# Float64 weights decoded and split between the steps of a three-stage attention and feed-forward kernel

## The chip, the cores and the metric

One core of a Trainium2 chip runs the whole kernel as one program. The metric is device time in microseconds (us). The kernel before took 1129.61 us, median of 3 runs (1129.01 to 1131.65). A profile of one execution of it is what the rows below are from.

## The reference

The inputs are an attention problem (B = 4, H = 8, S = 576, D = 64) and two feed-forward layers on its 2304 x 512 output, each with 512 x 2048 and 2048 x 512 weights (the first layer's `w_in` arrives scaled by 4.32). The weights are float64, so a core that computes in 32 bits has to decode them.

```
local   = softmax(causal(q k^T / 8)) v
mem_out = phi(q) M_prev / (phi(q) z_prev + 1e-6),  phi(x) = x if x > 0 else exp(x) - 1, plus 1
x = sigmoid(beta) * mem_out + (1 - sigmoid(beta)) * local
h = x @ w_in1;  g = h if h >= 1, 0 if h <= -1, else (h + 1)^2 / 4;  x = g @ w_out1
h = x @ w_in2;  g = max(0.01 h, h);                                out = g @ w_out2
```

## The kernel before

All products of the feed-forward layers run on TensorE (PE) in a reduced fp32 format. To keep precision, each operand is split into a high part and a low remainder: ScalarE (ACT) copies the value into the reduced format, VectorE (DVE) subtracts that from the value. Each product is then three matmuls: high x high, high x low, low x high.

A layer's 2048 hidden units do not fit in memory at once, so each layer is computed in two halves of 8 slots of 128 hidden units. That makes four segments (`SEGS`): 0 and 1 are layer 1, 2 and 3 are layer 2. Each segment goes over 9 chunks of 256 tokens (`CHUNKS`, 36 in all). The program counts time in steps: step x = 8n + f is chunk n, slot f. Layer 1 has steps 0 to 143. Layer 2 has a product step for each pair of slots (x = 144, 146, ...). Attention runs interleaved with the first 46 steps; behind it a block (`manual_schedule`) keeps TensorE, ScalarE, VectorE and GpSimd in the order in which the program is written. The DMA queue of SyncE (SP) is ordered by a planner.

A layer 1 step is `mm_h` (12 matmuls, then on ACT a Relu and a Square, L542 and L543, then on DVE the value g, its high part gh and its low part gl, L544 to L546), and `mm_y` of the step two before (`LAG` = 2: 12 matmuls on gh and gl). The last `mm_y` of a chunk is followed by `finish`, in segment 1 with two DVE adds (L569). At f = 5 the next chunk's x is split: `high_x` (L507 on DVE for layer 1, L509 on ACT for layer 2) and `low_x` (DVE, L514).

A layer 2 step is `mm_h2` (24 matmuls, then an ACT copy scaled by 0.01, L589, a DVE maximum, L590, and four DVE sums of 128 columns, L591 to L594, that feed a 7-product form of a 2x2 block multiplication), `layer2_y` of the step two before (21 matmuls, L607 to L609; after the fourth, `finish2` with 7 DVE adds), an ACT copy gh (L735) and the DVE remainder gl (L716).

Weights come as 64-bit integers in tiles `raw` (three buffers, 512 KB each). Decoding half a slot is one ACT operation (L122) and five DVE operations (L123, L127, L129, L130, L132). `split_half` splits a decoded input half (ACT L189, DVE L190). `split_out` first forms four combinations of two output halves on DVE (L204 to L207) and then splits them in two parts of two splits each; one of its temporaries, `t1`, is taken from the two buffers of g.

When all this is done stands in a table of jobs by step: `FETCH` for segment 1 (12 of its 16 decodes at steps 47, 49, ... 69), `HALVES` for segments 2 and 3, and a list of steps for the splits of segments 2 and 3. `do_jobs(x)` stands ahead of `mm_h` in layer 1, so a step's whole decode and its splits are ahead of that step's g in the DVE's queue:

```
for f in range(NSLOT):
    do_jobs(8 * n + f)
    pend.append((n, f, mm_h(n, f)))
```

In layer 2 `do_jobs(x - 1)` stands ahead of `mm_h2` and `do_jobs(x)` ahead of gl.

Of the kernel before, what the change touches and what calls it, by code (L numbers as in the profile page):

```python
# [20 lines left out]
TC = 256  # L21
# [15 lines left out]

BOOT, BOOT0, DELAY = 2.0, 12.0, 1.0

FETCH = {1: [24 + 4 * i for i in range(NW)] + [47 + 2 * i for i in range(16 - NW)]}  # L40
HALVES = {N1: [82 + 7 * i // 2 for i in range(16)], N1 + 1: [x for x in range(150, 209) if x % 8 in (0, 6)]}
HB = 1

# [8 lines left out]
def attn_moe_moe_kernel(ctx, tc, q, k, v, m_prev, z_prev, beta, w1i, w1o, w2i, w2o, out):  # L52
# [73 lines left out]
    def decode_b(lo, dst, a, r):  # L126
        nc.vector.scalar_tensor_tensor(out=a, in0=dst.bitcast(I32), scalar=3, in1=a,  # L127
                                       op0=ALU.logical_shift_left, op1=ALU.bitwise_or)
        nc.vector.tensor_scalar(out=r.bitcast(I32), in0=a, scalar1=-2 ** 23, scalar2=None, op0=ALU.bitwise_and)  # L129
        nc.vector.scalar_tensor_tensor(out=r, in0=lo.bitcast(U32), scalar=2.0 ** -52, in1=r,  # L130
                                       op0=ALU.mult, op1=ALU.mult)
        nc.vector.tensor_tensor(dst, a.bitcast(F32), r, ALU.add)  # L132

    slot_w, phase = {}, []
# [28 lines left out]
    def fetch_halves(seg, halves):  # L163

        ahead = 2 if seg else RAWB
        if any(SEGS[t][0:2] == SEGS[seg][0:2] for t in range(seg)):
            for k, (f, x) in enumerate(halves):
                nc.sync.dma_start(out=new_w32(seg, f, x, k), in_=w_d[f][:, x])
                yield
                yield  # L170
            return
        raws = [load_raw(seg, *h) for h in halves[0:ahead]]
        for k, (f, x) in enumerate(halves):
            if not raws:
                raws = [load_raw(seg, *h) for h in halves[k:k + ahead]]
            w32 = new_w32(seg, f, x, k if seg else 0)
            part = decode_a(raws.pop(0), w32)
            yield
            decode_b(*part)
            if any(SEGS[t][0:2] == SEGS[seg][0:2] for t in range(seg + 1, N1)):  # L180
                nc.sync.dma_start(out=w_d[f][:, x], in_=w32)
            else:
                raws += [load_raw(seg, *h) for h in halves[k + ahead:k + ahead + 1]]
            yield

    slots = {}

    def split(dst, src):
        nc.scalar.activation(dst[:, 0], src, AF.Copy)  # L189
        nc.vector.tensor_tensor(dst[:, 1], src, as_r(dst[:, 0]), ALU.subtract)  # L190

    def split_half(seg, f, x):
        w = wts.tile([128, 2, 512], F32R, tag="io"[x] + str(f), name="io"[x] + str(f))
        split(w, slot_w.pop((seg, f, x)))
        slots[f, x] = w

    def split_out(seg, p):


        a, b = (slot_w.pop((seg, f, 1)) for f in (2 * p, 2 * p + 1))  # L200
        b11, b12, b21, b22 = (x[:, c:c + 256] for x in (a, b) for c in (0, 256))
        t = l2_pool().tile([128, 3, 256], F32, tag="t", bufs=2, name="t")
        t1 = ffn.tile([128, TC], F32, tag="g", bufs=2, name="g")
        nc.vector.tensor_tensor(t1, b12, b11, ALU.subtract)  # L204
        nc.vector.tensor_tensor(t[:, 0], b22, t1, ALU.subtract)
        nc.vector.tensor_tensor(t[:, 1], b22, b12, ALU.subtract)
        nc.vector.tensor_tensor(t[:, 2], t[:, 0], b21, ALU.subtract)  # L207
        wa = wts.tile([128, 2, 512], F32R, tag=f"o{2 * p}", name="wa")
        wb = wts.tile([128, 2, 512], F32R, tag=f"o{2 * p + 1}", name="wb")
        ex = l2_pool().tile([128, 2, 768], F32R, tag=f"ex{p}", name="ex")  # L210
        split(wa[:, :, 0:256], b11)
        split(wb, b)
        yield
        split(wa[:, :, 256:512], t1)
        split(ex, t.rearrange("p i c -> p (i c)"))
        slots["out", p] = (wa, wb, ex)
        yield
# [285 lines left out]

    def high_x(n):
        xh = ffn.tile([128, 4, TC], F32R, tag="xh", bufs=2, name="xh")
        if SEGS[CHUNKS[n][0]][0] == 0:
            nc.vector.tensor_copy(xh, xin[n])  # L507
        else:
            nc.scalar.activation(xh, xin[n], AF.Copy)  # L509
        return xh  # L510
# [17 lines left out]
    def mm_h(n, f):  # L528
        seg, c = CHUNKS[n]
        w = slots[f, 0]  # L530
        xh, xl = xin[n]
        hp = psum()[:, 0:TC] if attended else ps.tile([128, TC], F32, tag="h", bufs=HB, name="h")
        for ct in range(4):
            wh, wl = w[:, 0, 128 * ct:128 * ct + 128], w[:, 1, 128 * ct:128 * ct + 128]
            nc.tensor.matmul(hp, wh, xh[:, ct], start=(ct == 0), stop=False)  # L535
            nc.tensor.matmul(hp, wh, xl[:, ct], start=False, stop=False)  # L536
            nc.tensor.matmul(hp, wl, xh[:, ct], start=False, stop=(ct == 3))  # L537
        g = ffn.tile([128, TC], F32, tag="g", bufs=2, name="g")
        gh = ffn.tile([128, TC], F32R, tag="gh", bufs=GB, name="gh")
        gl = ffn.tile([128, TC], F32R, tag="gl", bufs=GB, name="gl")  # L540

        nc.scalar.activation(g, hp, AF.Relu, bias=0.5, scale=0.5)  # L542
        nc.scalar.activation(g, g, AF.Square)  # L543
        nc.vector.scalar_tensor_tensor(out=g, in0=hp, scalar=1.0, in1=g, op0=ALU.max, op1=ALU.min)  # L544
        nc.vector.tensor_copy(gh, g)  # L545
        nc.vector.tensor_tensor(gl, g, as_r(gh), ALU.subtract)  # L546
        return gh, gl

    def mm_y(n, f, yp, gg):
# [24 lines left out]
    def mm_h2(n, p):  # L574


        ws = slots[2 * p, 0], slots[2 * p + 1, 0]
        xh, xl = xin[n]
        hp = psum()
        for s in range(2):  # L580
            o = hp[:, TC * s:TC * s + TC]
            for ct in range(4):
                wh, wl = ws[s][:, 0, 128 * ct:128 * ct + 128], ws[s][:, 1, 128 * ct:128 * ct + 128]
                nc.tensor.matmul(o, wh, xh[:, ct], start=(s == 0 and ct == 0), stop=False)  # L584
                nc.tensor.matmul(o, wh, xl[:, ct], start=False, stop=False)  # L585
                nc.tensor.matmul(o, wl, xh[:, ct], start=False, stop=(s == 1 and ct == 3))  # L586
        g = l2_pool().tile([128, 8, 128], F32, tag="g2", bufs=2, name="g2")
        h4 = hp.rearrange("p (a t) -> p a t", t=128)
        nc.scalar.activation(g[:, 4:8], h4, AF.Copy, scale=0.01)  # L589
        nc.vector.tensor_tensor(g[:, 0:4], h4, g[:, 4:8], ALU.max)  # L590
        nc.vector.tensor_tensor(g[:, 4], g[:, 0], g[:, 2], ALU.add)  # L591
        nc.vector.tensor_tensor(g[:, 6], g[:, 1], g[:, 0], ALU.subtract)
        nc.vector.tensor_tensor(g[:, 5], g[:, 4], g[:, 1], ALU.subtract)
        nc.vector.tensor_tensor(g[:, 7], g[:, 3], g[:, 5], ALU.subtract)  # L594
        gh = l2_pool().tile([128, 7, 128], F32R, tag="gh2", bufs=2, name="gh2")
        gl = l2_pool().tile([128, 7, 128], F32R, tag="gl2", bufs=2, name="gl2")
        return g, gh, gl
# [49 lines left out]
    def at_step(x, fn, *args):  # L647
        jobs.setdefault(x, []).append((fn, args))


    for seg in range(1, N1):
        x0 = START[seg]
# [1 line left out]
        part = fetch_halves(seg, [h[1:] for h in order])  # L654
        for i, (x, f, io) in enumerate(order):
            at_step(x, split_half, seg, f, io)
            at_step(FETCH[seg][i], next, part)
            at_step(FETCH[seg][i], next, part)
    for seg, xs in HALVES.items():
        part = fetch_halves(seg, [(f, x) for f in range(NSLOT) for x in range(2)])  # L660
        for x in xs:
            at_step(x - 1 if seg > N1 else x, next, part)
            at_step(x, next, part)
    for seg, xs in ((N1, (138, 140, 142, 144, 140, 142, 143.5, 144)), (N1 + 1, (210, 212, 214, 216, 214, 216, 220, 222))):
        for p in range(NSLOT // 2):
            for f in (2 * p, 2 * p + 1):
                at_step(xs[p], split_half, seg, f, 0)
            part = split_out(seg, p)
            at_step(xs[4 + p], next, part)
            at_step(int(xs[4 + p]) + 1, next, part)  # L670
# [16 lines left out]
    def layer1_steps():  # L687
        load_x(0)
        low_x(0, high_x(0))
        for n, (seg, c) in enumerate(CHUNKS):  # L690
            if SEGS[seg][0] == 1:
                break
            for f in range(NSLOT):
# [7 lines left out]
                    load_prev(n)  # L701
                if len(pend) > LAG:
                    layer1_y()
                yield 1

    def layer2_y():
# [9 lines left out]
        nc.vector.tensor_tensor(gl, g[:, 1:8], as_r(gh), ALU.subtract)  # L716

    def layer2():
        for n, (seg, c) in enumerate(CHUNKS):
            if SEGS[seg][0] == 0:  # L720
                continue
            for p in range(NSLOT // 2):
# [12 lines left out]
                nc.scalar.activation(gg[1], gg[0][:, 1:8], AF.Copy)  # L735
                if p == 2 and n + 1 < len(CHUNKS):
                    low_x(n + 1, xh)
                do_jobs(x)
                low_part(*gg)
                pend.append((n, p, gg))  # L740
                if p == 2 and n in again:
                    load_prev(n)
# [21 lines left out]
    def do_boot():  # L764
        while boot_jobs and boot_jobs[0][0] <= done:
            _, kind, f, io = boot_jobs.pop(0)
            with tc.issue_after(scored[0]) if scored[0] is not None else ExitStack():
                if kind == 0:
                    next(first), next(first)
                else:  # L770
                    split_half(0, f, io)

# [7 lines left out]

    with tc.manual_schedule(engines={nc.tensor.engine, nc.scalar.engine, nc.vector.engine, nc.gpsimd.engine}):
        attended = True
        for _ in steps:
            pass
        layer2()
# [25 lines left out]
```

## Time and profile before

| | |
|---|---|
| median of 3 runs | 1129.61 us |
| the profiled execution | 1128.14 us, of which 1126.4 us span from first to last instruction |
| PE busy | 1068.6 us (95%) |
| DVE busy | 913.2 us (81%) |
| ACT busy | 602.3 us (53%) |
| mean granted TensorE clock | 0.978 |

How to read it: busy time is a sum over stages. Attention fills the first 425 us, layer 1 reaches to about 719 us (some of it already beside attention), layer 2 to the end. In a table of stretches each line is a stretch (start:end, length), then busy time and (number of instructions) of PE, PEld (weight loads), DVE, ACT and POOL, then the granted TensorE clock, the DMA share and GB/s. In a timeline a line is start, duration, engine, source line, operation, output<-inputs, shapes, count, and in brackets the idle time before and what ended it. Durations overlap a little: the next independent instruction of an engine can start before the one ahead has ended, so what an instruction costs its queue is the distance from its start to the next start.

### The profile page before, as it was taken

What the parts mean: (1) busy time and instruction counts of PE and PEld (TensorE: products, weight loads), DVE (VectorE), ACT (ScalarE), POOL (GpSimd) and SP (SyncE); (2) the same over time, 40 slices, a digit from 0 to 9 for tenths busy, and PEclk for the clock granted to TensorE, in tenths of its full rate; (3) what the DMA queues carried; (4) which work ended last, traced back from release to release, by engine and by line L of the source; (5) the groups of instructions that cost most, each with busy time, mean ns of one, the idle gap of its engine ahead of it and who ended that gap; (6) DMA issues with size and microseconds to landing.
All of it is one profiled execution on the core that took longest, in us unless ns stands there. A gap on an engine that the chain in (4) does not pass through costs nothing.

```text
span 1126.4 us, 22350 instructions
## 1 busy us (share of the span) xinstructions
PE 1068.6 (95%) x8520; PEld 1008.8 (90%) x8520; DVE 913.2 (81%) x2327; ACT 602.3 (53%) x1368; POOL 29.0 (3%) x28
## 2 busy tenths in 40 slices
PE   5877899999999999999999999899999998999997
PEld 4656777888888889989999999899999998999997
DVE  6698999876677767996887877999998999877766
ACT  6998787666676754463333334544444464334332
POOL 0000000000000000000000000000000000211211
PEclk9887999999999999999999999999999999999999
DMA  6455554443344313431343434123322111311211
GB/s 147 115 158 160 147 143 142 119 115 68 88 93 114 81 34 105 133 113 56 127 136 95 132 113 132 57 76 128 97 95 95 58 38 38 113 57 57 98 53 57
DMA packets 122171, 112.09 MB, mean 100 GB/s; under 512 B 67280, under 2 KB 100048, under 8 KB 122064
## 3 DMA queue, kind: packets, MB, share of 16 engines
q1 hardware_dynamic: 122064, 110.66, 33.3%
q8 instruction: 67, 1.10, 0.4%
q14 instruction: 40, 0.33, 0.1%
HBM read 77.60 MB, written 23.59 MB: 90 GB/s over the span
## 4 chain that ended last, share of the span: by engine, by line
PE 75%; DVE 13%; ACT 5%; DMA 4%; issue 2%; SPq 1%; DVEq 0%; ACTq 0%
PE A L584 6%; PE A L585 6%; PE A L586 6%; PE y L557 4%; PE A L535 4%; PE y L556 4%; PE A L537 4%; PE A L536 4%; PE y L558 3%; PE y L609 3%; PE y L608 3%; PE y L607 3%; PE A L348 2%; PE h L535 2%; PE h L536 2%; PE h L537 2%
## 5 line engine op out<-in xcount | busy, mean ns | idle before, releaser
L584 PE MATMUL A<-xh,i 128*128 128x256 f32 x576 | 164.1, 285 | 0.0
L585 PE MATMUL A<-xl,i 128*128 128x256 f32 x576 | 164.0, 285 | 0.0
L586 PE MATMUL A<-xh,i 128*128 128x256 f32 x576 | 163.9, 285 | 0.0
L735 ACT ACTIVATE gh<-g 128x896 fp32r<-128x896 f32 x72 | 68.6, 953 | 145.5 <-DVE g L594 89.5
L542 ACT ACTIVATE g<-A 128x256 f32<-128x256 f32 x98 | 37.5, 383 | 166.3 <-PE A L537 146.0
L585 PEld LDWEIGHTS A<-xl,i 128*128 128x128 f32 x576 | 111.7, 194 | 0.0
L584 PEld LDWEIGHTS A<-xh,i 128*128 128x128 f32 x576 | 111.7, 194 | 0.0
L586 PEld LDWEIGHTS A<-xh,i 128*128 128x128 f32 x576 | 111.6, 194 | 0.0
L556 PE MATMUL y<-gh,o 128*128 128x256 f32 x384 | 108.0, 293 | 3.8 <-DVE gh L545 2.6
L535 PE MATMUL A<-xh,i 128*128 128x256 f32 x392 | 111.5, 284 | 0.0
L536 PE MATMUL A<-xl,i 128*128 128x256 f32 x392 | 111.3, 284 | 0.0
L537 PE MATMUL A<-xh,i 128*128 128x256 f32 x392 | 111.3, 284 | 0.0
L557 PE MATMUL y<-gl,o 128*128 128x256 f32 x384 | 110.1, 289 | 0.2
L558 PE MATMUL y<-gh,o 128*128 128x256 f32 x384 | 108.8, 286 | 0.0
L716 DVE TENSOR_TENSOR gl<-g,gh 128x896 fp32r<-128x896 f32 x72 | 86.8, 1205 | 19.8 <-ACT gh L735 19.8
L363 ACT ACTIVATE e<-e,mx 128x128 f32<-128x128 f32 (+2 forms) x144 | 84.2, 586 | 21.0 <-DVE mx L360 20.9
L360 DVE CUSTOM_DVE_ANT_0 e<-A,mask 128x384 f32<-128x384 f32 (+4 forms) x126 | 60.4, 483 | 42.7 <-PE A L348 41.5
L589 ACT ACTIVATE g<-A 128x512 f32<-128x512 f32 x72 | 42.8, 594 | 74.8 <-PE A L586 74.7
L556 PEld LDWEIGHTS y<-gh,o 128*128 128x128 f32 x384 | 72.0, 193 | 5.4 <-DVE gh L545 3.2
L535 PEld LDWEIGHTS A<-xh,i 128*128 128x128 f32 x392 | 75.8, 193 | 0.4 <-issue 0.4
L536 PEld LDWEIGHTS A<-xl,i 128*128 128x128 f32 x392 | 75.7, 193 | 0.0
L537 PEld LDWEIGHTS A<-xh,i 128*128 128x128 f32 x392 | 75.7, 193 | 0.0
(249 smaller groups left out, 3369.9 us busy)
## 6 DMA issues: line engine op xcount, KB each, us to landing
raw<-in_moe_w_in_dram SPq DMA_DIRECT2D x32, 512.0 KB, 3.7
raw<-in_moe_w_out_dram SPq DMA_DIRECT2D x32, 512.0 KB, 3.4
qk<-qk SPq DMA_DIRECT2D x64, 144.0 KB, 2.5
xf<-y_d SPq DMA_DIRECT2D x18, 512.0 KB, 4.1
xf<-x_d SPq DMA_DIRECT2D x12, 512.0 KB, 3.9
yp_d<-ys SPq DMA_DIRECT2D x18, 256.0 KB, 2.2
xf<-yp_d SPq DMA_DIRECT2D x9, 512.0 KB, 3.4
y_d<-ys SPq DMA_DIRECT2D x18, 256.0 KB, 2.1
```

The costliest lines, as they stand in the source:

```text
L363: nc.scalar.activation(e[:, 0:w], e[:, 0:w], AF.Exp, bias=mx, scale=-1.0, accum_out=ls[:, h:h + 1])
L535: nc.tensor.matmul(hp, wh, xh[:, ct], start=(ct == 0), stop=False)
L536: nc.tensor.matmul(hp, wh, xl[:, ct], start=False, stop=False)
L537: nc.tensor.matmul(hp, wl, xh[:, ct], start=False, stop=(ct == 3))
L556: nc.tensor.matmul(o, wh, gh, start=(f == 0 and et % 2 == 0), stop=False)
L557: nc.tensor.matmul(o, wh, gl, start=False, stop=False)
L558: nc.tensor.matmul(o, wl, gh, start=False, stop=(f == NSLOT - 1 and et % 2 == 1))
L584: nc.tensor.matmul(o, wh, xh[:, ct], start=(s == 0 and ct == 0), stop=False)
L585: nc.tensor.matmul(o, wh, xl[:, ct], start=False, stop=False)
L586: nc.tensor.matmul(o, wl, xh[:, ct], start=False, stop=(s == 1 and ct == 3))
L716: nc.vector.tensor_tensor(gl, g[:, 1:8], as_r(gh), ALU.subtract)
L735: nc.scalar.activation(gg[1], gg[0][:, 1:8], AF.Copy)
```

## The change

- **Decode in pieces.** `decode_b` yields after each DVE operation, so a decode is five pieces instead of two.
- **Filling.** In the part of layer 1 behind attention (`filling`), decode pieces and the DVE subtraction of `split` are not issued where the job stands. They go on a list (`between`), and `mm_h` takes one of them after each of g, gh and gl; `fill(99)` at the end of the step issues what is left. The ACT copies of splits stay where they were.
- **Steps.** The 12 late decodes of segment 1 move to steps 47 + 3i//2 (47, 48, 50, 51, ... 63). The splits of segment 2 move by up to 4 steps, one combination (p = 2) is done ahead at step 136. `do_jobs(x)` goes behind gl for x up to 146.
- **Combination.** `t1` is written in place over the decoded half; the tile t has three buffers.
- **ScalarE.** The layer 2 activation is one ACT operation (`Prelu`, alpha 0.01) in place of the ACT copy and the DVE maximum. `high_x` of layer 1 is on ACT once attention is over.

```diff
-FETCH = {1: [24 + 4 * i for i in range(NW)] + [47 + 2 * i for i in range(16 - NW)]}
+FETCH = {1: [24 + 4 * i for i in range(NW)] + [47 + 3 * i // 2 for i in range(16 - NW)]}
...
     def decode_b(lo, dst, a, r):
         nc.vector.scalar_tensor_tensor(out=a, in0=dst.bitcast(I32), scalar=3, in1=a,
                                        op0=ALU.logical_shift_left, op1=ALU.bitwise_or)
+        yield
         nc.vector.tensor_scalar(out=r.bitcast(I32), in0=a, scalar1=-2 ** 23, scalar2=None, op0=ALU.bitwise_and)
+        yield
...
+    between, filling = [], False
+
+    def fill(n=1):
+        while between and n:
+            fn, args = between.pop(0)
+            fn(*args)
+            n -= 1
+
     def split(dst, src):
         nc.scalar.activation(dst[:, 0], src, AF.Copy)
-        nc.vector.tensor_tensor(dst[:, 1], src, as_r(dst[:, 0]), ALU.subtract)
+        args = dict(out=dst[:, 1], in0=src, in1=as_r(dst[:, 0]), op=ALU.subtract)
+        if filling:
+            between.append((lambda: nc.vector.tensor_tensor(**args), ()))
+        else:
+            nc.vector.tensor_tensor(**args)
...
-        t1 = ffn.tile([128, TC], F32, tag="g", bufs=2, name="g")
-        nc.vector.tensor_tensor(t1, b12, b11, ALU.subtract)
-        nc.vector.tensor_tensor(t[:, 0], b22, t1, ALU.subtract)
         nc.vector.tensor_tensor(t[:, 1], b22, b12, ALU.subtract)
+        nc.vector.tensor_tensor(b12, b12, b11, ALU.subtract)
+        nc.vector.tensor_tensor(t[:, 0], b22, b12, ALU.subtract)
         nc.vector.tensor_tensor(t[:, 2], t[:, 0], b21, ALU.subtract)
+        combos[seg, p] = b11, b12, b, t
...
-        if SEGS[CHUNKS[n][0]][0] == 0:
+        if SEGS[CHUNKS[n][0]][0] == 0 and not attended:
             nc.vector.tensor_copy(xh, xin[n])
...
         nc.vector.scalar_tensor_tensor(out=g, in0=hp, scalar=1.0, in1=g, op0=ALU.max, op1=ALU.min)
+        fill()
         nc.vector.tensor_copy(gh, g)
+        fill()
         nc.vector.tensor_tensor(gl, g, as_r(gh), ALU.subtract)
+        fill()
...
-        nc.scalar.activation(g[:, 4:8], h4, AF.Copy, scale=0.01)
-        nc.vector.tensor_tensor(g[:, 0:4], h4, g[:, 4:8], ALU.max)
+        nc.scalar.activation(g[:, 0:4], h4, AF.Prelu, alpha=0.01)
...
-    for seg, xs in ((N1, (138, 140, 142, 144, 140, 142, 143.5, 144)), (N1 + 1, (210, 212, 214, 216, 214, 216, 220, 222))):
+    for seg, xs in ((N1, (138, 140, 143, 146, 141, 143.5, 146, 148)), (N1 + 1, (210, 212, 214, 216, 214, 216, 220, 222))):
...
+            if (seg, p) == (N1, 2):
+                at_step(136, combine, seg, p)
...
                 if len(pend) > LAG:
                     layer1_y()
+                fill(99)
                 yield 1
...
-                do_jobs(x)
+
+                if x > 146:
+                    do_jobs(x)
                 low_part(*gg)
+                if x <= 146:
+                    do_jobs(x)
```

## Rows read from the trace of the kernel before

**Rows 1.** The page's first part: busy time, share and instructions by engine.
```profile
PE 1068.6 (95%) x8520; PEld 1008.8 (90%) x8520; DVE 913.2 (81%) x2327; ACT 602.3 (53%) x1368; POOL 29.0 (3%) x28
```

**Rows 2.** Table of stretches: full-rate ones and the three short ones.
```profile
485.00:515.00 30.00, 27.47 (x208) 26.47 (x207) 28.22 (x59) 17.62 (x37) 0.00 (x0) 0.94 0.32 104
515.00:715.00 200.00, 200.00 (x1669) 200.00 (x1668) 155.08 (x338) 71.27 (x167) 0.00 (x0) 1.00 0.34 109
715.00:740.00 25.00, 20.68 (x148) 20.07 (x147) 22.54 (x49) 12.11 (x21) 0.00 (x0) 0.86 0.14 44
740.00:925.00 185.00, 185.00 (x1544) 185.00 (x1544) 171.96 (x367) 83.61 (x119) 0.00 (x0) 1.00 0.26 89
925.00:940.00 15.00, 11.18 (x79) 10.77 (x78) 14.65 (x32) 9.09 (x16) 0.00 (x0) 0.89 0.19 70
```

**Rows 3.** Waits of PE behind attention: waiter <- releaser: us in total, times, longest.
```profile
PE y L609 <- DVE gl L716: 4.2, 1, 4.2
PE h L607 <- DVE ys L634: 3.5, 1, 3.5
PE y L556 <- DVE gh L545: 2.4, 2, 1.5
```

**Rows 4.** Timeline of DVE: one decode and the g of a step.
```profile
459.98 0.42 DVE L123 TENSOR_SCALAR da<-raw 128x512 int32<-128x512 int32 x1
460.51 0.69 DVE L127 SCALAR_TENSOR_TENSOR da<-w32b,da 128x512 int32<-128x512 int32 x1
461.24 0.43 DVE L129 TENSOR_SCALAR dr<-da 128x512 int32<-128x512 int32 x1
...
463.03 0.42 DVE L544 SCALAR_TENSOR_TENSOR g<-A,g 128x256 f32<-128x256 f32 x1
463.55 0.29 DVE L545 CAST gh<-g 128x256 fp32r<-128x256 f32 x1
463.88 0.43 DVE L546 TENSOR_TENSOR gl<-g,gh 128x256 fp32r<-128x256 f32 x1
464.22 0.42 DVE L544 SCALAR_TENSOR_TENSOR g<-A,g 128x256 f32<-128x256 f32 x1
```

**Rows 5.** Groups of instructions by line: count, busy us, mean ns, idle before.
```profile
L543 ACT ACTIVATE g<-g 128x256 f32<-128x256 f32 x144 | 60.3, 419 | 3.8
L589 ACT ACTIVATE g<-A 128x512 f32<-128x512 f32 x72 | 42.8, 594 | 74.8 <-PE A L586 74.7
L514 DVE TENSOR_TENSOR xl<-xf,xh 128x1024 fp32r<-128x1024 f32 x36 | 43.9, 1220 | 0.4
L590 DVE TENSOR_TENSOR g<-A,g 128x512 f32<-128x512 f32 x72 | 49.5, 688 | 25.9 <-ACT g L589 25.7
```

**Rows 6.** The page's DMA issues: count, KB each, us from issue to landing.
```profile
raw<-in_moe_w_in_dram SPq DMA_DIRECT2D x32, 512.0 KB, 3.7
```

**Rows 7.** Timeline of DVE at the start of layer 2.
```profile
725.89 1.29 DVE L190 TENSOR_TENSOR i<-w,i 128x512 fp32r<-128x512 f32 x2
727.10 0.42 DVE L204 TENSOR_TENSOR g<-w 128x256 f32<-128x256 f32 x1
...
729.50 1.09 DVE L716 TENSOR_TENSOR gl<-g,gh 128x896 fp32r<-128x896 f32 x1
730.50 0.42 DVE L190 TENSOR_TENSOR wa<-g,wa 128x256 fp32r<-128x256 f32 x1
...
731.70 0.69 DVE L590 TENSOR_TENSOR g<-A,g 128x512 f32<-128x512 f32 x1
...
733.16 0.29 DVE L594 TENSOR_TENSOR g<-g 128x128 f32<-128x128 f32 x1
```

**Rows 8.** Timeline of DVE in the stretch before the wait for L634.
```profile
930.47 0.42 DVE L622 TENSOR_TENSOR s<-s 128x256 f32<-128x256 f32 x1
...
933.25 1.08 DVE L716 TENSOR_TENSOR gl<-g,gh 128x896 fp32r<-128x896 f32 x1
```

**Rows 9.** Timeline of ACT: the only table load.
```profile
0.73 1.28 ACT L80 ACT_TABLE_LOAD   x1 [0.73 <-PEq L798]
```

More of the change, by code (lines that the diff above doesn't have):

```diff
@@ L128, in decode_b @@
                                        op0=ALU.logical_shift_left, op1=ALU.bitwise_or)
+        yield
         nc.vector.tensor_scalar(out=r.bitcast(I32), in0=a, scalar1=-2 ** 23, scalar2=None, op0=ALU.bitwise_and)
+        yield
         nc.vector.scalar_tensor_tensor(out=r, in0=lo.bitcast(U32), scalar=2.0 ** -52, in1=r,
                                        op0=ALU.mult, op1=ALU.mult)
+        yield
         nc.vector.tensor_tensor(dst, a.bitcast(F32), r, ALU.add)
@@ L168, in fetch_halves @@
                 nc.sync.dma_start(out=new_w32(seg, f, x, k), in_=w_d[f][:, x])
-                yield
-                yield
+                for _ in range(5):
+                    yield
             return
@@ L178, in fetch_halves @@
             yield
-            decode_b(*part)
+            yield from decode_b(*part)
             if any(SEGS[t][0:2] == SEGS[seg][0:2] for t in range(seg + 1, N1)):
@@ L195, in split_half, with combine, split_out @@
         slots[f, x] = w
-    def split_out(seg, p):
+    combos = {}
+    def combine(seg, p):
         a, b = (slot_w.pop((seg, f, 1)) for f in (2 * p, 2 * p + 1))
         b11, b12, b21, b22 = (x[:, c:c + 256] for x in (a, b) for c in (0, 256))
-        t = l2_pool().tile([128, 3, 256], F32, tag="t", bufs=2, name="t")
-        t1 = ffn.tile([128, TC], F32, tag="g", bufs=2, name="g")
-        nc.vector.tensor_tensor(t1, b12, b11, ALU.subtract)
-        nc.vector.tensor_tensor(t[:, 0], b22, t1, ALU.subtract)
+        t = l2_pool().tile([128, 3, 256], F32, tag="t", bufs=3, name="t")
         nc.vector.tensor_tensor(t[:, 1], b22, b12, ALU.subtract)
+        nc.vector.tensor_tensor(b12, b12, b11, ALU.subtract)
+        nc.vector.tensor_tensor(t[:, 0], b22, b12, ALU.subtract)
         nc.vector.tensor_tensor(t[:, 2], t[:, 0], b21, ALU.subtract)
+        combos[seg, p] = b11, b12, b, t
+    def split_out(seg, p):
+        if (seg, p) not in combos:
+            combine(seg, p)
+        b11, t1, b, t = combos.pop((seg, p))
         wa = wts.tile([128, 2, 512], F32R, tag=f"o{2 * p}", name="wa")
@@ L648, in at_step, with piece @@
         jobs.setdefault(x, []).append((fn, args))
+    def piece(part):
+        if filling:
+            between.append((next, (part,)))
+        else:
+            next(part)
     for seg in range(1, N1):
@@ L656, in attn_moe_moe_kernel @@
             at_step(x, split_half, seg, f, io)
-            at_step(FETCH[seg][i], next, part)
-            at_step(FETCH[seg][i], next, part)
+            for _ in range(5):
+                at_step(FETCH[seg][i], piece, part)
     for seg, xs in HALVES.items():
@@ L662, in attn_moe_moe_kernel @@
             at_step(x - 1 if seg > N1 else x, next, part)
-            at_step(x, next, part)
-    for seg, xs in ((N1, (138, 140, 142, 144, 140, 142, 143.5, 144)), (N1 + 1, (210, 212, 214, 216, 214, 216, 220, 222))):
+            for _ in range(4):
+                at_step(x, piece, part)
+    for seg, xs in ((N1, (138, 140, 143, 146, 141, 143.5, 146, 148)), (N1 + 1, (210, 212, 214, 216, 214, 216, 220, 222))):
         for p in range(NSLOT // 2):
@@ L718, in layer2 @@
     def layer2():
+        nonlocal filling
+        filling = False
         for n, (seg, c) in enumerate(CHUNKS):
@@ L768, in do_boot @@
                 if kind == 0:
-                    next(first), next(first)
+                    for _ in range(5):
+                        next(first)
                 else:
@@ L782, in attn_moe_moe_kernel @@
         attended = True
+        filling = True
         for _ in steps:
```

## The prediction

> **What bounds the kernel now.** I read the busy shares first. PE is busy 95% of the span, DVE 81%, ACT 53% [rows 1], so only time that PE loses can be given back. Next the table of stretches, as a rate: from 515 to 715 us PE starts 1669 matmuls in 200 us, 8.345 per us or 0.1198 us each, and from 740 to 925 us 1544 in 185 us, again 8.346, both at clock 1.00 [rows 2]. Behind attention PE thus runs at one rate and falls short of it in three stretches. At 8.345 per us, 485 to 515 us should hold 250.4 matmuls and holds 208, 715 to 740 us 208.6 against 148, and 925 to 940 us 125.2 against 79 [rows 2]. The gaps are 42.4, 60.6 and 46.2 matmuls, or 5.1, 7.3 and 5.5 us, together **17.9 us**. The list of PE's waits names who was late, and it is DVE each time: gh of layer 1 (2.4 us), the first gl of layer 2 (4.2 us), and the adds at the end of a chunk that free a PSUM bank (3.5 us) [rows 3]. The waits sum to 10.1 us. Most of the other 7.8 us is the clock: it is granted at 0.94, 0.86 and 0.89 in these stretches, an average of full speed (2.4 GHz) and the lower level (1.2 GHz), and at 1.00 in the long stretches where PE never waits [rows 2]. Each us of stall therefore costs about 1.8 us. Attention and the end of the program (PE's last matmuls to the last store) run the same instructions in the same order after the change, and I leave them as they are.
>
> **Decodes between g, 485 to 515 us.** Before, a decode costs DVE 3.04 us from start to start (459.98 to the g that starts at 463.03) and a g, gh, gl chain 1.19 us (463.03 to 464.22) [rows 4]. The distances show a second thing. Where an instruction needs the one just ahead, the next start comes after the duration: 0.53 us behind L123 of 0.42, 0.73 behind L127 of 0.69, 0.52 behind L544 of 0.42, 0.33 behind L545 of 0.29. Where it does not, the next start comes 0.08 us before the end: 0.34 behind L546 of 0.43 [rows 4]. Put between each other, L544, L545, L123 and L127 all get an independent neighbour and cost 0.34, 0.21, 0.34 and 0.61, which saves 0.18 + 0.12 + 0.19 + 0.12 = 0.6 us in each step with a decode. Such a step then costs DVE 4.23 - 0.6 = 3.63 us, a plain one 1.19, one at f = 5 another 1.2 for xl [rows 4, 5]; the cast xh leaves DVE.
>
> A layer 1 step is 24 matmuls, 2.875 us of PE. The new steps put two decodes into every three steps, so I carry DVE's backlog: after 47 and 48 it is 2 x (3.63 - 2.875) = 1.5 us, step 49 clears it, and 50 to 52 repeat that. Step 53 has xl too: 1.96, then 2.7 after 54 and 1.0 after 55; 2.5 after 57, 0.85 after 58, 2.4 after 60, 1.9 after 61 (xl, no decode), 3.4 after 63. From 65 the splits come, with no decode beside them: at most two per step, 1.19 + 1.2 = 2.4 us, under PE's 2.875, and the backlog goes. How much PE lets pass: from the end of the products of step f to the first use of its gh lie four half steps, 4 x 12 x 0.1198 = 5.75 us. ACT's two activations of 256 columns take 0.42 us each [rows 5], some 0.9 with the start. A plain step then needs 1.19 us more, so 3.6 us are free; in a step with a decode gl has L123 and L127 ahead of it and is late 1.9 us behind the start, so 2.9 us are free. The largest backlogs at the start of a step are 3.4 (step 64, plain) and 2.6 (step 63): both pass, by 0.2 to 0.3 us. I expect nearly all of the 5.1 us back and keep 0.9 for the near miss. If the overlap does not come, the first rival has the price.
>
> The moved jobs issue a 512 KB load behind each decode, 3.7 us to landing [rows 6]. Three buffers make that load needed no sooner than three decodes later, four steps or 11.5 us less one decode, so SP's queue, which the loads share with x and the stores, has some 4 us to spare. The ACT copy L122 now stands behind Square and not ahead of Relu; an ACT copy of 512 columns takes 0.594 us [rows 5], so it is done when L127 comes up 0.9 us later.
>
> **Start of layer 2, 715 to 740 us.** Before, DVE reaches the first gl (L716) at 729.50, behind a combination, its splits and two input splits, while PE waits 4.2 us [rows 3, 7]. Costs from the same rows: two input splits 1.21 us, combination and first half of an output split 2.40, gl 1.00, second half 1.20, maximum with sums 1.75, of which the sums are 1.02 (731.70 to the end of L594 less 0.73 for L590) [rows 7]. After the change I count from T, the end of the products of step 143 on PE. PE: h2 of the first step ends at T + 4.3, the second (behind the last two layer 1 outputs) at 10.1, the third at 12.9, and the first output products start there. DVE, with 0.9 us of backlog from 141 to 143: g of step 143 and two splits to 4.2, combination and first half of p = 1 to 6.6, sums to 7.6, two adds of the last layer 1 chunk of at most 0.69 each [rows 5] to 9.0, gl to 10.0. That is 2.9 us before PE wants it, where it was 4.2 late. Second half to 11.2, sums 12.2, a wait of 1.0 for gh (an estimate from 0.594 us for 512 columns [rows 5]; gh has 896), gl to 14.2, splits of p = 3 to 15.4 (PE starts on them at 15.5, on the second at 16.9), output splits of p = 2 to 17.5, sums 18.5, xl 19.7, combination p = 3 22.1, gl 23.1 (wanted at 23.7), then 24.3, sums and a decode to 28.2, gl 29.2 (wanted at 29.1). From there the jobs are few. The order holds with nothing to spare at two places, so I keep 0.9 of the 7.3 us.
>
> **ScalarE activation, 925 to 940 us.** L590 goes, 72 x 0.688 = 49.5 us of DVE's time [rows 5]. In layer 2 at full rate PE hides DVE anyway (171.96 of 185 us busy, no loss) [rows 2], so most of that buys nothing. It counts in the steps 210 to 224, where the second half's splits come on top. Per product step (45 matmuls, 5.39 us) DVE has 2.02 us of sums and gl, 2.78 us for the chunk's adds every fourth step [rows 8], 1.2 for xl, and the splits of rows 7. The sums: 6.0, 4.4, 5.6, 6.8, 6.0, 5.6, 5.6, 3.2 us. Backlog: 0.6, 0, 0.2, 1.6, 2.2, 2.4, 2.6, 0.4. With L590, 0.73 more per step, it was 1.35, 1.1, 2.1, 4.2 when the adds of step 218 came up, and there PE waited 3.5 us [rows 3]. The adds are now 2.6 us earlier by the backlog and 0.73 by their own step, 3.3 against 3.5 of wait. I keep 0.9 of 5.5 us. The Prelu itself has no row: the ACT copy it replaces has the same shape and takes 0.594 us [rows 5], the nearest below is 0.42 (256 columns), above 0.594 + 1.28 if a table load came with it [rows 9]. I take 0.594; its chain also loses the step through DVE.
>
> **Sum.** 17.9 us less 3 x 0.9 = 15.2 us. The profiled execution took 1128.14 us, 1.74 around its span of 1126.4, and stands 1.47 below the median of 1129.61. So 1126.4 becomes 1111.2 and the median **1114.4 us**. What the edits add elsewhere is covered: the xh copies on ACT, about 1 us in eight steps, by ACT's 71 of 200 us [rows 2].
>
> **Rivals.**
> 1. *The new decode steps overload DVE* (10%). For: DVE is busy 28.2 of 30 us in that stretch [rows 2], and 3.63 us rests on the overlap alone. Without it, steps 47 to 63 need 12 x 3.04 + 17 x 1.19 + 2 x 1.2 = 59.1 us against 17 x 2.875 = 48.9 of PE, 10.2 over; less 3 us of slack 7.2 us of stall, times 1.8 for the clock up to 13. In place of the 5.1 lost now that leaves 17.9 - 1.8 - 7.2 to 13, a gain of 3 to 9 us: 1121 to 1127. Against: DVE's rows show the overlap for every kind of operation.
> 2. *The two places at the start of layer 2, or the chunk's adds at 218, stay late* (15%). For: gl comes 0.1 us after PE wants it. Some 1 to 2 us of stall each at 1.8 leave 4 to 7 us: 1116 to 1120, middle 1118.
> 3. *Slower: a table switch at each activation* (5%). Until now ACT has loaded one table, for 1.28 us [rows 9], and Exp, Relu, Square and Copy ran on it. If Prelu is not beside Copy, ACT switches twice per product step, at L589's place and at L735. ACT is busy 83.61 of 185 us [rows 2], 2.44 us per step of 5.39, so it decides from (5.39 - 2.44) / 2 = 1.47 us per switch. At 1.28 it hides; at twice 1.28 each step takes 7.56 us, 72 x 2.17 = 156 us more: 1270. Against: four functions shared one load. The Trainium skill (ScalarE: Activation LUTs, What ACT_TABLE_LOAD costs) has a load at 1283 ns, which this trace agrees with (1.28), and a drain of 1380 ns with each switch, which no run here shows; 2.66 us would be beyond 1.47. Its section Table sets says that cheap functions are in every set, and that Prelu is one of them it does not say.
> 4. *No change* (2%): the waits only move to the next late instruction.
>
> **How the numbers follow.** My forecast, 1111.7 (all 17.9 us back) to 1117, has 68%. With rival 2 and half of rival 1 the range 1111.5 to 1121.5 holds some 8 in 10 and a little more. A measurement here can tell about 0.2%, 2.3 us: forecast and rivals 1 and 2 are faster (0.92, with 0.01 off for the upper end of rival 1), no change 0.03, slower 0.05.
>
> **What would show it.** Clock 1.00 and 8.345 matmuls per us in the three stretches; no L716 or L634 among PE's waits; about 3.6 us of DVE per decode step, with L123 and L127 between L544 and L546; L590 gone and its 49.5 us of DVE time; one table load. Wrong would be a PE wait for gh or gl in steps 47 to 64 (rival 1), for gl behind 725 us (rival 2), or a table load in layer 2 (rival 3).

## The result and the profile after

The changed kernel took **1114.26 us** (median of 4 runs, 1111.81 to 1116.02) against 1130.63 for the kernel before (4 runs, 1129.01 to 1133.31): ratio 0.9851, 95% interval 0.9822 to 0.9881, so 1.5% faster. The forecast was 1114.4 us. Medians repeat less closely than these two numbers agree (the four runs span 4 us). The profiled execution took 1113.12 us, with a span of 1111.3 where 1111.2 was forecast.

The page's busy line of the changed kernel, to be read beside [rows 1]:

```profile
PE 1060.2 (95%) x8520; PEld 1002.1 (90%) x8520; DVE 851.4 (77%) x2244; ACT 612.4 (55%) x1379; POOL 28.9 (3%) x28
```

DVE is busy 61.8 us less, of which L590 was 49.5 [rows 5]. PE does the same 8520 matmuls.

The table of stretches of the changed kernel, cut as in [rows 2] with two more lines around 750 and 915 us:

```profile
485.00:515.00 30.00, 30.00 (x253) 30.00 (x252) 21.63 (x50) 18.86 (x40) 0.00 (x0) 1.00 0.20 68
515.00:715.00 200.00, 200.00 (x1669) 200.00 (x1668) 145.74 (x339) 78.66 (x174) 0.00 (x0) 1.00 0.34 109
715.00:740.00 25.00, 24.91 (x206) 24.53 (x205) 22.39 (x47) 14.72 (x26) 0.00 (x0) 1.00 0.27 85
740.00:760.00 20.00, 18.69 (x156) 18.49 (x156) 18.78 (x41) 8.50 (x12) 0.00 (x0) 1.00 0.40 134
900.00:925.00 25.00, 23.80 (x199) 23.60 (x198) 24.04 (x56) 15.14 (x27) 0.00 (x0) 1.00 0.15 54
925.00:940.00 15.00, 15.00 (x128) 15.00 (x127) 13.52 (x33) 8.64 (x14) 0.00 (x0) 1.00 0.04 14
```

At 8.345 matmuls per us the first stretch is full (253 of 250), the start of layer 2 lacks 2.6 (0.3 us), and 740 to 760 and 900 to 925 us lack 10.9 and 9.6 (1.3 and 1.2 us). The clock is 1.00 in all of them. Of 17.9 us, 2.8 are left.

PE's waits behind attention, all of them (compare [rows 3]):

```profile
PE h L632 <- DVE ys L659: 2.5, 2, 1.3
```

gh (L556 before) and gl (L609 before) are gone from the list. What is left is the bank that the chunk's adds free, once at the first chunk of layer 2 and once at step 218.

**A measure for the experiments.** Whole runs of one kernel differ by 4 us (the four runs of the changed kernel) to 9 us (1126.09 to 1134.73, the kernel before beside e5 to e8), and some of that comes before the part that the change touches: attention's last wide matmul starts at 427.5 us in one profile and as late as 432.6 in another. I therefore also read the time from that matmul to PE's last one. Kernel before:

```profile
427.46 0.27 PE L436 MATMUL A<-pb,vn 128*64 128x128 f32 x1
...
1118.92 0.28 PE L609 MATMUL A<-ex,gl 128*128 128x256 f32 x1
```

Changed kernel:

```profile
427.76 0.27 PE L459 MATMUL A<-pb,vn 128*64 128x128 f32 x1
...
1103.91 0.28 PE L634 MATMUL A<-ex,gl 128*128 128x256 f32 x1
```

That is 691.46 and 676.15 us, 15.3 us apart. Behind the last matmul come 7.5 and 7.4 us in both. A second profile of the changed kernel (e9) gave 676.16, and the two profiles of e8 and e10, one kernel, gave 673.84 and 673.86: in these pairs the distance repeats to 0.02 us, much closer than whole runs do.

### The profile page after: what moved, and what is told of

Same layout as the page of the kernel before. It is cut to its first block, busy times and chain, and to the rows that moved or that the text cites. A ratio compares the mean times of both kernels' runs of the same rounds, so it can differ in the third digit from the quotient of the medians.

```text
span 1111.3 us, 22273 instructions
## 1 busy us (share of the span) xinstructions
PE 1060.2 (95%) x8520; PEld 1002.1 (90%) x8520; DVE 851.4 (77%) x2244; ACT 612.4 (55%) x1379; POOL 28.9 (3%) x28
## 4 chain that ended last, share of the span: by engine, by line
PE 81%; DVE 9%; DMA 4%; ACT 3%; issue 1%; SPq 1%; DVEq 0%; ACTq 0%
PE A L612 6%; PE A L611 6%; PE A L610 6%; PE A L558 4%; PE A L560 4%; PE A L559 4%; PE y L582 4%; PE y L583 4%; PE y L584 4%; PE y L634 3%; PE y L633 3%; PE y L632 3%; PE A L371 3%; PE A L423 2%; PE h L558 2%; PE h L559 2%
## 5 line engine op out<-in xcount | busy, mean ns | idle before, releaser
L567 DVE SCALAR_TENSOR_TENSOR g<-A,g 128x256 f32<-128x256 f32 x98 | 41.3, 422 | 55.6 <-ACT g L566 55.0
```

## The experiments

All were timed in five rounds against the kernel before. That kernel took 1130.63 us beside the changed kernel, 1131.88 beside e1 to e4, 1132.38 beside e5 to e8 and 1131.37 beside e9 and e10. So runs are compared by their ratios, and a median can lie 1 to 2 us above a range that was worked out from the first result. "Distance" is the measure just described, from one profile of each run.

| run | median us | ratio to before, 95% | distance us | to its parent |
|---|---|---|---|---|
| before | 1130.63 | | 691.46 | |
| changed | 1114.26 | 0.9851 (0.9822 to 0.9881) | 676.15 | -15.3 |
| e1 Prelu alone | 1125.43 | 0.9938 (0.9919 to 0.9957) | 686.44 | -5.0 to before |
| e2 all but Prelu | 1126.55 | 0.9954 (0.9937 to 0.9971) | 686.28 | +10.1 to changed |
| e3 jobs ahead of g | 1124.80 | 0.9938 (0.9918 to 0.9958) | 683.33 | +7.2 |
| e4 jobs behind gl | 1122.74 | 0.9925 (0.9904 to 0.9946) | 683.69 | +7.5 |
| e5 old steps of splits | 1121.82 | 0.9903 (0.9875 to 0.9931) | 680.77 | +4.6 |
| e6 xh on DVE | 1117.43 | 0.9875 (0.9850 to 0.9900) | 676.79 | +0.6 |
| e7 old fetch steps | 1118.85 | 0.9888 (0.9863 to 0.9912) | 678.43 | +2.3 |
| e8 bank copied | 1114.44 | 0.9843 (0.9817 to 0.9870) | 673.84 | -2.3 |
| e9 changed again | 1114.82 | 0.9866 (0.9842 to 0.9891) | 676.16 | 0.0 |
| e10 bank copied again | 1113.76 | 0.9856 (0.9832 to 0.9879) | 673.86 | -2.3 |

**e1, Prelu alone.**

```diff
# on the kernel before
-        nc.scalar.activation(g[:, 4:8], h4, AF.Copy, scale=0.01)
-        nc.vector.tensor_tensor(g[:, 0:4], h4, g[:, 4:8], ALU.max)
+        nc.scalar.activation(g[:, 0:4], h4, AF.Prelu, alpha=0.01)
```

> The kernel before, with one edit: the layer 2 activation is one ACT operation and L590 is gone. Theory (DVE's backlog at 210 to 224 is what L590 costs): the stretch 925 to 940 us gets back 4 of its 5.5 us, the start of layer 2 about 1.3 of 7.3 (one maximum less ahead of the first gl), the first stretch keeps its 5.1: about 1125 us, 5.3 less than before. Rival (PE hides DVE in layer 2 anyway): 1130 us, all three stretches as they were.

Measured 1125.43 us. PE's waits, to be read beside [rows 3]:

```profile
PE y L608 <- DVE gl L715: 3.5, 1, 3.5
PE y L556 <- DVE gh L545: 2.4, 2, 1.5
PE h L606 <- DVE ys L633: 1.2, 1, 1.2
```

The wait of the adds falls from 3.5 to 1.2 us, that for the first gl from 4.2 to 3.5, which is the 0.7 us of one maximum, and layer 1's is unchanged. The theory holds where the most was expected of it: from 900 to 950 us e1 has 407 matmuls and the kernel before 371, 4.3 us. The start of layer 2 gives back little, 443 matmuls against 440 from 700 to 760 us, 0.4 us where 1.3 was expected. The rival falls: L590 was hidden in most of layer 2 and not at 210 to 224.

**e2, all but Prelu** (the same three lines, taken back in the changed kernel).

> The changed kernel with the ACT copy and the DVE maximum back. If the parts add up, it is slower by what the part alone gave, 5 us: 1119.5 us. Theory: more than that, 1121 to 1124 us, because the new steps at the start of layer 2 hold with no time to spare (gl of the fourth product step 0.1 us late by my count) and three maxima are 2.2 us there. Rival (L590 was hidden): 1114 to 1115 us.

Measured 1126.55 us, distance +10.1: twice what the part gives alone, and a little beyond my range. PE's waits:

```profile
PE h L633 <- DVE ys L660: 6.5, 3, 3.5
PE y L635 <- DVE gl L752: 1.1, 1, 1.1
PE A L612 <- DVE i L206: 0.8, 1, 0.8
PE y L633 <- ACT s L645: 0.3, 1, 0.3
```

From 900 to 950 us it has 371 matmuls and the changed kernel 407 (4.3 us), from 700 to 760 us 441 against 485 (5.3 us). The second number is the one the part alone does not show. The waits there are for an input split, for gl and for the adds of the first chunk: the later steps of the splits move DVE's work into the first product steps of layer 2, and there is room for it there only because each maximum is gone.

**e3, jobs ahead of g.**

```diff
# on the changed kernel, ahead of the steps behind attention
-        filling = True
+        filling = False
```

> The changed kernel with the filling off: at the new steps, all pieces of a decode and the splits stand ahead of g again. Theory (a decode between those of g costs DVE 0.6 us less, 3.63 and not 4.23 us a step, and the new steps need that): 7.2 us of stall in steps 47 to 64, 1 to 1.8 times that in all, 1121 to 1127 us, with PE waits on gh or gl there. Rival (the pieces only change places, DVE does the same work): 1114 to 1116 us.

**e4, jobs behind gl.**

```diff
         nc.vector.scalar_tensor_tensor(out=g, in0=hp, scalar=1.0, in1=g, op0=ALU.max, op1=ALU.min)
-        fill()
         nc.vector.tensor_copy(gh, g)
-        fill()
         nc.vector.tensor_tensor(gl, g, as_r(gh), ALU.subtract)
-        fill()
```

> The changed kernel with the three single fills in the step's g chain taken out: all pieces come behind gl. g is then ahead of the decode, but no instruction of the two lies between those of the other. Theory (what counts is DVE's time, 4.23 us a step as in e3): 1120 to 1127 us, close to e3. Rival (what counts is that g no longer waits behind a decode): 1114 to 1116 us, as the changed kernel.

The two answer one question. The stretch of the new decode steps, in e3:

```profile
450.00:495.00 45.00, 40.78 (x318) 38.55 (x317) 40.94 (x88) 19.48 (x41) 0.00 (x0) 1.00 0.47 143
```

and in e4:

```profile
450.00:495.00 45.00, 41.65 (x320) 39.01 (x319) 41.33 (x88) 21.08 (x44) 0.00 (x0) 1.00 0.47 145
```

375.5 matmuls are due, 318 and 320 came: 6.9 and 6.7 us. DVE is busy 91 and 92% of the stretch, PE waits for gh in five and six places of 0.2 to 1.6 us. From one g to the next, DVE's timeline has, with no idle time between, in e3

```profile
450.98 0.42 DVE L567 SCALAR_TENSOR_TENSOR g<-A,g 128x256 f32<-128x256 f32 x1
...
455.22 0.42 DVE L567 SCALAR_TENSOR_TENSOR g<-A,g 128x256 f32<-128x256 f32 x1
```

and in e4

```profile
458.47 0.42 DVE L567 SCALAR_TENSOR_TENSOR g<-A,g 128x256 f32<-128x256 f32 x1
...
462.71 0.42 DVE L567 SCALAR_TENSOR_TENSOR g<-A,g 128x256 f32<-128x256 f32 x1
```

That is 4.24 us in both, where the changed kernel takes 3.60 for the same eight instructions (its lines stand below). Whether the decode stands ahead of g or behind gl makes almost no difference; that its instructions do not lie between those of g costs 7 us. So the gain of the filling is DVE's time, and not that g comes sooner. e4 also waits 0.8 us for an input split at the start of layer 2, which is part of its +7.5. The forecast for the absence of the filling was 7.2 us of stall, times 1 to 1.8. What is missing is 6.9 and 6.7 us, so the factor was 1, at clock 1.00.

**e5, old steps of the splits.**

```diff
-(N1, (138, 140, 143, 146, 141, 143.5, 146, 148))
+(N1, (138, 140, 142, 144, 140, 142, 143.5, 144))
...
-            if (seg, p) == (N1, 2):
-                at_step(136, combine, seg, p)
...
+                do_jobs(x)
-                if x > 146:
-                    do_jobs(x)
                 low_part(*gg)
-                if x <= 146:
-                    do_jobs(x)
```

> The changed kernel with the old steps of segment 2's splits, no combination ahead at 136, and the jobs ahead of gl at 144 and 146 as before. Theory (the first gl of layer 2 stands behind a combination and its splits, 4.2 us late before, 0.73 less without the maximum): a stall of some 3.5 us at the start of layer 2, with the clock 4 to 6 us: 1118 to 1120.5 us. Rival (the DVE time that filling and Prelu free is enough): 1114 to 1115 us.

Distance +4.6, as expected (4 to 6 us). The median, 1121.82 us, is above the range by 1.3, but the kernel before took 1.75 us more beside this run than beside the changed kernel. Its waits:

```profile
PE y L634 <- DVE gl L749: 3.9, 1, 3.9
PE h L632 <- DVE ys L659: 1.2, 1, 1.2
```

The wait for the first gl is back, at 3.9 us (expected 3.5). Filling and Prelu do not make the new steps unnecessary. From 700 to 760 us the kernel before starts 440 matmuls, e1 443, e2 441, e5 446 and the changed kernel 485: at the start of layer 2 neither the new steps nor Prelu gains as much as 1 us without the other.

**e6, xh on DVE.**

```diff
-        if SEGS[CHUNKS[n][0]][0] == 0 and not attended:
+        if SEGS[CHUNKS[n][0]][0] == 0:
```

> The changed kernel with the cast xh of layer 1 on DVE again (0.72 us more in steps 53 and 61). Theory by the backlog count: it is 4.1 at the start of step 63 and 4.8 at 64, where 2.9 and 3.6 pass, so PE stalls about 1.2 us there and the run takes 1.2 to 2.2 us more: 1115.5 to 1116.5 us, with a PE wait on gh or gl near 480 us. Rival (there is more slack than I count): no wait, 1114.3 us.

There is one wait more, in the output products of step 63, where the count had put it (later than 480 us, as attention ends 3.7 us later in this profile). PE's timeline:

```profile
487.20 0.38 PE L583 MATMUL h<-gl,o 128*128 128x256 f32 x1 [0.46 <-DVE gl L571]
```

It costs 0.6 us of distance, not 1.2: the slack is about 0.6 us more than I counted. The median (1117.43) is within the noise of attention and says nothing on that.

**e7, old fetch steps.**

```diff
-FETCH = {1: [24 + 4 * i for i in range(NW)] + [47 + 3 * i // 2 for i in range(16 - NW)]}
+FETCH = {1: [24 + 4 * i for i in range(NW)] + [47 + 2 * i for i in range(16 - NW)]}
```

> The changed kernel with segment 1's late decodes at their old steps (47, 49, ... 69), still filled in between those of g. Theory by the backlog count: none up to 64, then decodes and splits meet: 2.0 after 67, 1.5 after 68, 4.6 after 69 (a decode, two splits and xl), so PE stalls about 1 us at step 70: 1115.3 to 1116.3 us. Rival A (filling alone is enough): 1114.3 us. Rival B (the new steps are the whole gain of that stretch): 1119 us.

PE's waits in that part, both in the output products of step 70, whose g stands behind the crowd of step 69 in DVE's queue:

```profile
505.56 0.38 PE L582 MATMUL y<-gh,o 128*128 128x256 f32 x1 [1.20 <-DVE gh L569]
506.50 0.39 PE L583 MATMUL y<-gl,o 128*128 128x256 f32 x1 [0.55 <-DVE gl L571]
```

The second wait is a price of the filling itself, for a split stands between gh and gl of that step:

```profile
505.22 0.29 DVE L569 CAST gh<-g 128x256 fp32r<-128x256 f32 x1
505.42 0.68 DVE L204 TENSOR_TENSOR i<-w32b,i 128x512 fp32r<-128x512 f32 x1
506.02 0.42 DVE L571 TENSOR_TENSOR gl<-g,gh 128x256 fp32r<-128x256 f32 x1
```

Distance +2.3, where 1 to 2 was expected; rivals A and B both fall. Together with e3 this gives the whole table of the first stretch: old steps without filling lose 5.1 us (the kernel before, which also has xh on DVE, and the lower clock in its loss), new steps without filling 7.2, old steps with filling 2.3, new steps with filling nothing.

**e8, bank copied.**

```diff
         nc.scalar.activation(s1, yp[1], AF.Copy)
-        p2, p3, p4 = yp[2][:, 0], yp[2][:, 1], yp[3][:, 0]
+        s2 = l2_pool().tile([128, 256], F32, tag="s2", name="s2")
+        nc.scalar.activation(s2, yp[2][:, 1], AF.Copy)
+        p2, p3, p4 = yp[2][:, 0], s2, yp[3][:, 0]
+        if n < len(CHUNKS) - 1:
+            tt(hi[:, 0:256], p2, s0[:, 0], ALU.add)
...
-        tt(hi[:, 0:256], p2, s0[:, 0], ALU.add)
+        if last:
+            tt(hi[:, 0:256], p2, s0[:, 0], ALU.add)
```

> The changed kernel, and in finish2 one half of the third bank is copied to SBUF by ACT, the add on its other half goes first, so that the bank is free after one of the seven adds and not after six. Theory (PE's two waits for L659, 2.5 us, are all that is left of the three stretches): 2.2 to 2.5 us less than the changed kernel, 1111.8 us, no L659 among PE's waits. Rival (the next late instruction, gl or a weight split, takes the place): 1113.5 to 1114.3 us.

In its profile PE waits for nothing that the list names behind attention. It runs at the full rate from there to 715 us, and from 715 to 1100 us holds 3200 matmuls where 3213 are due, 1.5 us short in gaps too small for the list:

```profile
425.00:715.00 290.00, 290.00 (x2420) 288.52 (x2418) 219.75 (x505) 127.86 (x283) 0.00 (x0) 1.00 0.36 113
715.00:1100.00 385.00, 384.71 (x3200) 383.93 (x3199) 299.92 (x636) 176.72 (x264) 27.13 (x16) 1.00 0.24 79
```

The distance is 2.3 us shorter, as expected. The median did not move (1114.44), and taken alone it would speak for the rival. Attention ended 3.0 us later in its one profile; whether it did so in the other runs is not shown. To tell these apart, both ran once more side by side.

**e9 and e10, the changed kernel and e8 again.**

> The changed kernel unaltered, beside e10 on the same chip and against the same runs of the kernel before. If the medians of e1 to e8 differ from their stretches behind attention only by where attention ends (427 to 433 us in these profiles), this gives a ratio of 0.985 to 0.988 again and 676 us from the last attention matmul to the last matmul, within 0.5 us.

> e8 unaltered, beside e9. Theory (the bank copy is worth its 2.3 us of stretch): a ratio 0.002 below e9's, and 673.8 us from the last attention matmul to the last matmul. Rival (it gives the 2.3 us back in attention or at the end): the same ratio as e9.

The distances came out as before, 676.16 and 673.86 us. The ratios are 0.9866 and 0.9856; the difference has the expected sign and half of the size, and the intervals overlap. That e10 is 2.3 us better behind attention is shown by the traces; that a whole run is faster is not resolved by these times.

## Why the prediction was right, step by step

- **The bound.** PE's rate of 8.345 matmuls per us with three gaps of 17.9 us was the right account: with the bank copy of e8 on top the distance is 17.6 us shorter than before, and PE waits in no place that the list names. The list of PE's waits was read with one line left out, 0.3 us for an ACT copy in the third stretch (y L607 <- s L619), so it was not DVE each time, and the waits sum to 10.4 us.
- **Decodes between g.** Forecast: 3.63 us of DVE per step with a decode, backlog up to 3.4 us, no wait. DVE's timeline of the changed kernel, step 47 and the start of 48:

```profile
431.91 0.42 DVE L567 SCALAR_TENSOR_TENSOR g<-A,g 128x256 f32<-128x256 f32 x1 [1.55 <-ACT g L566]
432.25 0.42 DVE L123 TENSOR_SCALAR da<-raw 128x512 int32<-128x512 int32 x1
432.58 0.29 DVE L569 CAST gh<-g 128x256 fp32r<-128x256 f32 x1
432.78 0.69 DVE L127 SCALAR_TENSOR_TENSOR da<-w32b,da 128x512 int32<-128x512 int32 x1
433.38 0.42 DVE L571 TENSOR_TENSOR gl<-g,gh 128x256 fp32r<-128x256 f32 x1
433.72 0.42 DVE L130 TENSOR_SCALAR dr<-da 128x512 int32<-128x512 int32 x1
434.17 0.69 DVE L132 SCALAR_TENSOR_TENSOR dr<-raw,dr 128x512 f32<-128x512 uint32 x1
434.90 0.69 DVE L135 TENSOR_TENSOR w32b<-da,dr 128x512 f32<-128x512 f32 x1
435.51 0.42 DVE L567 SCALAR_TENSOR_TENSOR g<-A,g 128x256 f32<-128x256 f32 x1
```

  3.60 us from g to g. The starts after L567, L123, L569 and L127 come 0.34, 0.33, 0.20 and 0.60 us later, where adjacent dependent ones had 0.52, 0.53, 0.33 and 0.73 [rows 4]. All 5.1 us came back; the 0.9 kept for a near miss was not needed, and e3 and e4 show that the overlap carries it. Rival 1 was their case, 7 us.
- **Start of layer 2.** Counted from T (707.32 us here), gl of the four product steps was forecast to end at 10.0, 14.2, 23.1 and 29.2. The changed kernel's DVE timeline:

```profile
715.40 1.08 DVE L751 TENSOR_TENSOR gl<-g,gh 128x896 fp32r<-128x896 f32 x1
...
720.61 1.09 DVE L751 TENSOR_TENSOR gl<-g,gh 128x896 fp32r<-128x896 f32 x1 [1.36 <-ACT gh L772]
...
722.55 1.28 DVE L206 TENSOR_TENSOR i<-w,i 128x512 fp32r<-128x512 f32 x2
...
730.07 1.08 DVE L751 TENSOR_TENSOR gl<-g,gh 128x896 fp32r<-128x896 f32 x1
...
736.05 1.08 DVE L751 TENSOR_TENSOR gl<-g,gh 128x896 fp32r<-128x896 f32 x1
```

  The next instructions start at about T + 9.1, 14.3, 23.7 and 29.7. PE's first output products start at 720.28, T + 13.0 (forecast 12.9). Two small errors: the input splits of p = 3 come behind the first half of p = 2 and not ahead of it (a loss of 0.3 us with gl of the fourth step), and I left out the adds of that chunk, which run into the same crowd; PE waits there 1.3 us. Kept were 0.9 us, lost 0.3 + 1.3.
- **ScalarE activation.** Its forecast share at 210 to 224 was 5.5 - 0.9 = 4.6 us; e1 shows 4.3 from the matmul counts (371 to 407 in 900 to 950 us), and 1.2 us of wait stays at step 218, the place named. The adds came 2.3 us earlier (a wait of 1.2 us left of 3.5), where 3.3 was counted. The count for the start of layer 2 left the maxima out too, but I did not see that this part of the gain hangs on Prelu: 5.3 us more in e2. The Prelu's own duration and the table loads of the changed kernel, by line:

```profile
L615 ACT ACTIVATE g<-A 128x512 f32<-128x512 f32 x72 | 42.8, 594 | 88.8 <-PE A L612 88.8
...
L80 ACT ACT_TABLE_LOAD x1 | 1.3, 1283 | 0.7 <-PEq L841 0.7
```

  594 ns, the copy's own, and still one load: rival 3 falls. The Trainium skill (ScalarE: Activation LUTs, Rules for kernel authors) sends max and relu to VectorE, which it has as up to about 3 times faster per element in bf16. Here, in fp32, the same 512 columns take 0.594 us on ACT and 0.688 on DVE [rows 5], and what decides is neither: DVE was the late engine, and ACT was busy 53% of the span [rows 1].
- **A size that was off.** I took 1.8 us of loss for each us of wait, from the lower clock in the three stretches of before. Most of the 7.8 us beyond the waits is the clock indeed. Behind the long waits of before PE's starts lie 0.21 us apart and not 0.12:

```profile
505.65 0.41 PE L535 MATMUL A<-xh,i 128*128 128x256 f32 x1
505.87 0.41 PE L536 MATMUL A<-xl,i 128*128 128x256 f32 x1
```

  There are 17, 25 and 17 such distances in the three stretches, each up to 0.09 us longer than at the full rate, which makes 1.5, 2.3 and 1.5 us (an estimate from the starts). The rest lies beside the waits. But 1.8 is no price that can be carried over. In the changed kernel the two waits for L659 cost about themselves (2.5 us listed, 2.5 missing). In e3 3.8 us are listed from 450 to 495 us and 6.9 missing, 1.8 again, yet at clock 1.00. PE's timeline shows why:

```profile
470.43 0.28 PE L560 MATMUL A<-xh,i 128*128 128x256 f32 x1
471.14 0.38 PE L582 MATMUL h<-gh,o 128*128 128x256 f32 x1 [0.43 <-DVE gh L569]
471.60 0.38 PE L583 MATMUL h<-gl,o 128*128 128x256 f32 x1
471.82 0.28 PE L584 MATMUL h<-gh,o 128*128 128x256 f32 x1
```

  These three distances are 0.71, 0.46 and 0.22 us where PE's rate is 0.12, so 1.03 us are lost and 0.43 listed: behind a late gh, gl is late too, and a gap that is little longer than a matmul's own 0.38 us has no idle time in brackets. This touched only the rivals' prices, since the forecast counted missing matmuls. Rival 1's 7.2 us were counted from DVE's time and are the whole loss already, so nothing was to be multiplied.
- **The sum.** Left over: 0 + 0.3 + 1.3 + 1.2 = 2.8 us, where 3 x 0.9 = 2.7 was kept. That the two agree so well is partly luck: no place lost its 0.9, the first lost nothing, the second 1.6 and the third 1.2.

## What to carry to other kernels

Read the distance between starts, not durations. In these traces a DVE instruction costs its queue 0.1 to 0.2 us more when the next one reads its result than when the next one does not, so two dependent chains woven into each other were cheaper than one behind the other (0.6 of 4.2 us). Do the same for PE: the wait that a list names can be half of what is lost around it. When the bound engine waits only in a few places, count what is missing from its rate there, carry the feeding engine's backlog step by step, and check each deadline. Parts of a schedule that fill each other's gaps do not add up: one part was worth 5 us alone and 10 in company.

## What the runs showed of the hardware that was not expected

- Waits of similar length had different clocks behind them. In the kernel before, two waits of 0.9 and 1.5 us stand in a stretch at 0.94; in e3 five waits of up to 1.56 us, and in e7 1.20 and 0.55 us close together, left it at 1.00. Each single wait of 3.5 us and more (before, e1, e2, e5) had a lower clock behind it, 0.86 in the 25 us from 715 or 0.89 in the 15 us from 925, and so had one of 2.65 us in e2 (0.91 from 740 to 760 us). What else decides was not tried.
- The time at which attention ends differs by up to 5 us between profiles (427.5 to 432.6 us), and by 1.4 us between two profiles of the same changed kernel, while the 676 us behind it repeat to 0.02 us. Why attention varies is open.
